# Four edits at once in a convolution and expert-lookup kernel: row halves in the first transform, a last quarter in two parts, fifteen score columns, and an index spread in two row tiles

## The chip, the cores and the metric

The kernel runs on one core of one Trainium2 chip. A core has a matrix engine (TensorE, PE in the profile, with its weight loads listed apart as PEld), a vector engine (VectorE, DVE), a scalar engine (ScalarE, ACT), a general engine (GpSimd, POOL), and a queue engine (SyncE, SP) that issues nearly all transfers of this kernel. The engines run their own instruction streams in order and wait for each other by semaphores. The metric is the device time of one execution in microseconds (us); lower is better.

## What is computed

The input is one sequence of 2048 positions with 512 channels. Two blocks follow each other, each on the normalised result of the one before, each added to its input:

```python
# block A: a state-space model as a long convolution
P = exp((A * dt)[:, :, None] * pos);  K = 2 * einsum("dn,dnl->dl", C, P).real
y = irfft(rfft(u, 2L) * rfft(K, 2L))[:L] + u * D_skip
# block B: 32 heads look up one of 256 experts for each position
q1, q2 = split(x @ w_q)                       # per head, 128 + 128
s1, s2 = q1 @ k1.T, q2 @ k2.T                 # 16 scores each
i1, i2 = argmax(s1), argmax(s2);  e = 16 * i1 + i2
out = sum over heads of gelu(x . u[e]) * v[e] # one candidate: the softmax is 1
```

## The kernel before

The program is a list of steps. Each step is added to a plan (`Plan.add`) with an engine, a cost, a function that issues its instructions, and the keys of data that it reads and writes. The order in which the steps are issued is the long tuple `ORDER`, written out by hand or by a search; the costs and lags in the plan do not act on the chip. Within an engine the steps run in the order of `ORDER`.

**Block A** handles the channels in four quarters, c = 0 to 3, and each quarter in four pieces kt.

- *Tables.* For each of 32 steps i, POOL makes phases (`phases`, L551) and magnitudes (`mags` L582, `tails` L588), with `steps`, `bases`, `powers` and `heads` once in four steps. ACT takes sines and cosines of the phases (L638 to L641), DVE multiplies (L645 to L658), and PE forms the convolution kernel from them (`kgen`, L684, tile `kps`). The tables have two buffers each, so `mags(i)` on POOL waits until `kgen(i-2)` has read its own.
- *Transforms.* `stage1` (L456 to L468) is the first factor of a Fourier transform, for the input (`u_s1`, tile `s1u`) and for the kernel (`k_s1`, tile `s1k`). For a piece it has two halves n. In each, for four g and two k, a matmul takes 128 rows of data (64 columns) as weights and moves `c1_s[:, k]`, 128 columns, of which only a block diagonal of four is not zero; k = 0 and 1 go to output partitions 0 to 63 and 64 to 127. ACT copies the bank out. `stage2` (L471 to L485, tiles `s2yu`, `s2yk`) is the second factor: eight steps k4 for a quarter, four matmuls of 128 x 128 weights and 128 columns each. `k_s2` multiplies the two spectra (DVE, L726 to L729; in the last quarter ACT, DVE and POOL share it, L733 and L737), and `k_ia` is the first inverse factor, eight steps n, 16 matmul records each (L758), copied to the tile `T` on ACT (in the last quarter ACT and DVE). In `k_s2` all eight steps wait for all four pieces of stage 1, and in `k_ia` all eight wait for all eight products.
- `yk` of one quarter takes the buffer that `yk` of the quarter before leaves after its `k_ia`.

**Between the blocks.** `w_piece(n)`, n = 0 to 31, multiplies the query weights with the keys `ka_s`, `kb_s` (load `wq`, L816; PE L822; turned by PE L830; ACT copies L826 and L834) and stores the product `w_d` in DRAM after every fourth piece (L837). It is read back as four tiles `w_q` and split into a high and a low part `w_hi`, `w_lo` (L914 to L918).

**Block B** goes through eight batches b of 256 positions: `inverse` (last inverse factor, L1029, then `h`), `center` and `variance`, `scores` for two halves of 128 positions, and `select`. In `scores`, four steps q of six matmuls give 1024 columns: 64 groups (32 heads, two keys) of 16 (L1143). DVE takes the maximum of each group (`top`, L1165), compares (`same`, L1169), multiplies the hits with powers of two (`weigh`, L1174); POOL adds the 16 up (`gather`, L1180); DVE reads the index from the exponent (`index`, L1187 to L1191). `select` turns the index of 32 heads (`ixt`, L1231), spreads it to 128 partitions by matmuls with the selector `sel` (`bc`, L1247: two matmuls of 32 rows for each of four banks), copies it out on ACT (L1251), compares it with the expert numbers on DVE (`oh`, L1269), counts (`cnt`, L1279) and multiplies with the values (`o`, L1316).

Of the kernel before, what the change touches and what calls it, by code (L numbers as in the profile page):

```python
# [9 lines left out]
F32 = mybir.dt.float32  # L10
# [9 lines left out]
P = 128  # L20
# [7 lines left out]
def view(t, off, dims):  # L28
# [135 lines left out]
def kernel(ctx, tc, xa, xb, xt, lar, aim, cre, cim, ldt, dsk, wq, ka, kb, ue, ve,  # L164
# [628 lines left out]
    def w_piece(n):  # L793
# [42 lines left out]
        def store():  # L836
            nc.sync.dma_start(w_d[:, :, 128 * hg:128 * hg + 128], W[hg])  # L837
# [598 lines left out]
```

## Time and profile before

| | |
|---|---|
| three runs | 508.86, 515.67 (median), 516.54 us |
| the profiled execution | 516.5 us, of which 514.7 us lie between the first and the last instruction (the span) |
| mean granted TensorE clock | 0.977 |
| busy, share of the span | PE 89%, DVE 80%, POOL 63%, ACT 58% |

A row of a group gives line, engine, operation, what is written and read, and the count; behind the bar stand the busy time of the group in us and the mean of one in ns, then the engine's idle time before them and what ended it. Matmuls overlap, so the mean of one is longer than the pace. Rows of the timeline and of the chain of waits give start, duration, and how many instructions they merge. A float32 matmul has two records on PE, each with a weight load on PEld. Rows of a table by stretch of time give, for each engine, busy time and number of instructions; then the granted clock, the share of the DMA engines and their rate.

### The profile page before, as it was taken

What the parts mean: (1) busy time and instruction counts of PE and PEld (TensorE: products, weight loads), DVE (VectorE), ACT (ScalarE), POOL (GpSimd) and SP (SyncE); (2) the same over time, 40 slices, a digit from 0 to 9 for tenths busy, and PEclk for the clock granted to TensorE, in tenths of its full rate; (3) what the DMA queues carried; (4) which work ended last, traced back from release to release, by engine and by line L of the source; (5) the groups of instructions that cost most, each with busy time, mean ns of one, the idle gap of its engine ahead of it and who ended that gap; (6) DMA issues with size and microseconds to landing.
All of it is one profiled execution on the core that took longest, in us unless ns stands there. A gap on an engine that the chain in (4) does not pass through costs nothing.

```text
span 514.7 us, 16728 instructions
## 1 busy us (share of the span) xinstructions
PE 459.3 (89%) x7206; PEld 392.3 (76%) x7206; DVE 411.3 (80%) x724; ACT 300.4 (58%) x596; POOL 321.7 (63%) x342
## 2 busy tenths in 40 slices
PE   0275889999999999999998949999999999999995
PEld 0143669888998999899997947877878888786784
DVE  5999898899959988999727573888969596979983
ACT  4867799967897598858964442334152341426240
POOL 4989979999999999996807011760351506263330
PEclk9998699999999999999999998999999999999998
DMA  7969474224043102611056984400162141010012
GB/s 255 385 206 383 127 276 146 65 84 175 3 177 96 40 3 82 202 50 44 1 208 183 292 266 155 144 1 1 54 186 91 30 137 42 1 43 0 2 42 85
DMA packets 27362, 61.32 MB, mean 119 GB/s; under 512 B 2932, under 2 KB 14456, under 8 KB 26136
## 3 DMA queue, kind: packets, MB, share of 16 engines
q1 hardware_dynamic: 27136, 60.11, 34.8%
q8 instruction: 57, 0.93, 0.8%
q10 hardware_dynamic: 152, 0.13, 0.1%
q14 instruction: 17, 0.14, 0.1%
HBM read 46.21 MB, written 14.02 MB: 117 GB/s over the span
## 4 chain that ended last, share of the span: by engine, by line
PE 62%; DVE 15%; ACT 11%; DMA 5%; issue 4%; POOL 2%; SPq 0%; DVEq 0%; ACTq 0%; POOLq 0%
PE sc L1143 18%; PE ia L758 8%; PE s2yk L482 4%; PE kps L684 4%; PE s1k L465 3%; PE xu L1150 3%; PE s2yu L482 3%; PE o L1316 3%; PE cnt L1279 3%; PE s1u L465 2%; PE ib L1029 2%; DMA wq<-wq 2%; ACT t L641 2%; PE bc L1247 1%; ACT t L639 1%
## 5 line engine op out<-in xcount | busy, mean ns | idle before, releaser
L551 POOL TENSOR_TENSOR pg<-PS 128x1024 int32<-128x1024 int32 x32 | 68.9, 2152 | 0.5
L582 POOL TENSOR_TENSOR mg<-TS 128x1024 f32<-128x1024 f32 x32 | 62.6, 1958 | 7.8 <-PE kps L684 4.1
L1180 POOL TENSOR_TENSOR ks<-kq 128x512 f32<-128x512 bf16 x16 | 18.9, 1182 | 56.6 <-DVE kq L1174 53.4
L1269 DVE TENSOR_SCALAR oh<-idxb,ec_s 128x2048 bf16<-128x2048 bf16 (+1 forms) x72 | 46.3, 708 | 8.9 <-ACT idxb L1251 7.0
L758 PE MATMUL ia<-ca_s,U 128*128 128x128 f32 x256 | 49.6, 276 | 0.0
L1053 POOL TENSOR_TENSOR vs<-hc 128x256 f32<-128x256 f32 x8 | 6.5, 815 | 62.5 <-ACT hc L1076 62.5
L1143 PE MATMUL sc<-w_hi,hhi 128*128 128x512 f32 x128 | 45.1, 434 | 0.0
L639 ACT ACTIVATE t<-t,halfpi 128x512 f32<-128x512 f32 x64 | 42.4, 662 | 2.1
L1143 PE MATMUL sc<-w_lo,hhi 128*128 128x512 f32 x128 | 40.8, 400 | 0.0
L638 ACT ACTIVATE t<-pg 128x512 f32<-128x512 int32 x64 | 38.9, 608 | 3.0 <-DVE gf L646 2.0
L1143 PE MATMUL sc<-w_hi,hlo 128*128 128x512 f32 x128 | 40.6, 399 | 0.0
L641 ACT ACTIVATE t<-pg 128x512 f32<-128x512 int32 x64 | 38.2, 608 | 3.2 <-POOL pg L551 2.1
L758 PEld LDWEIGHTS ia<-ca_s,U 128*128 128x128 f32 x256 | 38.9, 192 | 0.0
L758 PE MATMUL ia<-ca_s,yk 128*128 128x128 f32 x192 | 38.2, 281 | 0.4 <-DVE mg L658 0.4
L588 POOL TENSOR_TENSOR mg<-TS 128x512 f32<-128x512 f32 x32 | 37.4, 1171 | 0.4
L684 PE MATMUL kps<-mg 128*32 128x64 f32 x1024 | 34.0, 231 | 3.3 <-DVE mg L658 1.6
L465 PE MATMUL s1u<-c_s,xs 128*64 128x128 f32 x512 | 33.4, 277 | 2.5 <-DVE xs L502 1.6
L482 PE MATMUL s2yk<-yk,c_s 128*128 128x128 f32 x256 | 35.0, 283 | 0.5 <-DVE U L729 0.4
L684 PE MATMUL kps<-gf 128*32 128x64 f32 x1024 | 33.5, 228 | 0.9 <-issue 0.9
L482 PEld LDWEIGHTS s2yk<-yk,c_s 128*128 128x128 f32 x256 | 30.8, 192 | 3.7 <-issue 1.4
L465 PE MATMUL s1k<-c_s,k 128*64 128x128 f32 x512 | 32.8, 284 | 0.3 <-ACT yk L468 0.3
L482 PE MATMUL s2yu<-yu,c_s 128*128 128x128 f32 x256 | 32.6, 279 | 0.3
(197 smaller groups left out, 1380.9 us busy)
## 6 DMA issues: line engine op xcount, KB each, us to landing
wq<-wq SPq DMA_DIRECT2D x25, 512.0 KB, 4.1
t_d<-T SPq DMA_DIRECT2D x24, 256.0 KB, 4.2
Tb<-t_d SPq DMA_DIRECT2D x8, 768.0 KB, 6.0
x<-xa SPq DMA_DIRECT2D x8, 512.0 KB, 6.0
xs<-xb SPq DMA_DIRECT2D x16, 256.0 KB, 4.8
xt<-xt SPq DMA_DIRECT2D x8, 512.0 KB, 3.9
out<-ob SPq DMA_DIRECT2D x7, 512.0 KB, 3.0
c_s<-wq SPq DMA_DIRECT2D x4, 512.0 KB, 8.4
```

The lines of the kernel that those rows point to most:

```text
L465: T.matmul(ps[64 * k:64 * k + 64, g, :], lhs8(4 * n + g), c1_s[:, k], start=True, stop=True)
L482: T.matmul(ps[:, k, :], c2_s[:, kk, :], y[:, :, kk, :], start=True, stop=True)
L551: G.tensor_tensor(view(pg, 0, [[32, 2 * NC], [8, 4], [1, 8]]), view(t["PS"], 1024 + off, [[1, 2 * NC], [128, 4], [0, 8]]), view(t["PS"], 8 ...
L582: G.tensor_tensor(view(mg, 0, [[96, NC], [8, 8], [1, 8]]), view(ts, 512 + 8 * o, [[8, NC], [1, 8], [0, 8]]), view(ts, 8 * o, [[8, NC], [0, ...
L588: G.tensor_tensor(view(mg, 64, [[96, NC], [8, 4], [1, 8]]), view(ts, 1536 + o, [[1, NC], [64, 4], [0, 8]]), view(ts, 1024 + 8 * o, [[8, NC ...
L638: A.activation(p, pg[:, :, k], AF.Abs)
L639: A.activation(p, p, AF.Sin, scale=-SINSCALE, bias=halfpi)
L641: A.activation(p, pg[:, :, k], AF.Sin, scale=SINSCALE)
L684: T.matmul(kps[32 * q:32 * q + 32, 2 * g + h, :], m[:, d, 64:96], m[:, d, 0:64], start=(e == 0), stop=(e == 1))
L758: T.matmul(ps[:, g, :], t[:, 4 * n + g].rearrange("p a b -> p (a b)"), ca_s[:, s, :], start=(s == 0), stop=(s == 1))
L1143: T.matmul(ps[:, 512 * h:512 * h + 512], t[x_][:, q, ts], I[w_][:, q, 512 * h:512 * h + 512], start=(q == 0 and x_ == w_), stop=(q == 3 an ...
L1269: V.tensor_scalar(oh[:, :, 0:ln], t["idxb"][:, :, sl], S["ec"][:, 4 * e + j:4 * e + j + 1], None, op0=ALU.is_equal)
```

## The change

- **Stage 1 in row halves.** `c1_s` has 64 columns for each k in place of 128, a block diagonal of two. Each matmul of 128 rows becomes two of 64 rows (rows 0 to 63 and 64 to 127, h = 0 and 1), each moving 64 columns into its own bank. A piece takes both banks at once, and ACT copies each bank out after both halves of g.
- **The last quarter in two parts** (`SEGS = (1, 1, 1, 2)`). For c = 3, the steps k4 = 0 to 3 of `k_s2` handle the first two pieces kt and 4 to 7 the last two. A step has eight matmuls with 64 columns each in place of four with 128. `k_ia(3)` waits in its first four steps for the first four products alone.
- **Fifteen score columns.** POOL subtracts key 15 from the other fifteen (`differ`, two new operations that wait for the load of `ka_s`, `kb_s`), so the score of key 15 is zero and its column is dropped: 960 columns in place of 1024, matmuls of 480. DVE takes the larger of the maximum and zero (a new operation on 128 x 64), and the index formula is bounded from below so that no hit means 15. `gather` adds 0 to 7 and 7 to 14 with the weight of 7 halved.
- **Index spread in two row tiles.** `index` writes the index twice (64 columns), it is turned to 64 partitions, `sel` has two copies, and the eight matmuls of a batch come in two steps that alternate between rows 0 to 31 and 32 to 63, each with two banks.
- `ORDER` is new as a whole: 1712 steps in place of 1727. The keys of `params` were made stricter (`keyed`), which acts on the order alone. Some plan costs differ.

In the new `ORDER`, the weight pieces 26 to 31 stand ahead of `kgen(25)`; before, they stood among and behind the `s2yk` steps of the last quarter, ahead of `k_ia(3)`. In the last quarter the PE order is: stage 1 of kt 1, 0, 2; `kgen(30)`; `s2yk` 0 and 1; `kgen(31)`; `s2yk` 3; stage 1 of kt 3; `s2yk` 2, 4, 6, 5, 7; the eight `k_ia`. At the start, `aim` is loaded after the other five parameters (it was second), POOL begins with `differ`, `powers(0)`, `mags(1)`, and PE has weight pieces 0 to 10 ahead of `kgen(0)` (0 to 5, 7 and 9 before), 11 and 12 ahead of `kgen(1)`, up to 16 ahead of `kgen(2)` and up to 18 ahead of `kgen(3)`.

```diff
+        def differ():
+            for t, o in ((ka_s, 0), (kb_s, 16)):
+                G.tensor_tensor(t[:, o:o + 15], t[:, o:o + 15], t[:, o + 15:o + 16].to_broadcast([P, 15]), op=ALU.subtract)
+        plan.add("POOL", 0.6, differ, w=["ka"])
...
     def stage1(dst, lhs8, kt, nm, r, tiles, key):
...
-                ps = bank(job, f"{nm}_{n}")
-                for g in range(4):
+                if n == 0:
+                    for h in range(2):
+                        bank(job, f"{nm}_{h}", h)
+                for g in range(4 * n, 4 * n + 4):
                     for k in range(2):
-                        T.matmul(ps[64 * k:64 * k + 64, g, :], lhs8(4 * n + g), c1_s[:, k], start=True, stop=True)
+                        for h in range(2):
+                            hs = slice(64 * h, 64 * h + 64)
+                            T.matmul(flat(job[h], 64)[64 * k:64 * k + 64, g], lhs8(g)[hs], c1_s[hs, k], start=True, stop=True)
...
     def k_s2(c):
+        ns = SEGS[c]
         for k4 in range(8):
+            sg, nk = k4 * ns // 8, 4 * ns
+            g_, k_ = slice(32 * sg // ns, 32 * (sg + 1) // ns), slice(nk * (k4 % (8 // ns)), nk * (k4 % (8 // ns)) + nk)
+            kts = range(4 * sg // ns, 4 * (sg + 1) // ns)
...
+                for kk in range(k_.start, k_.stop):
+                    T.matmul(ps[:, kk - k_.start, :], c2_s[:, kk, :], spectrum(c, "yk")[:, g_, kk, :], start=True, stop=True)
...
-                    T.matmul(ps[:, 512 * h:512 * h + 512], t[x_][:, q, ts], I[w_][:, q, 512 * h:512 * h + 512],
+                    T.matmul(ps[:, 512 * h:512 * h + 480], t[x_][:, q, ts], I[w_][:, q, 480 * h:480 * h + 480],
...
+            V.tensor_scalar_max(d["mx"], d["mx"], 0.0)
+            V.tensor_tensor(eq, ps, d["mx"].rearrange("p (b g) -> p b g", b=2).unsqueeze(3).to_broadcast([P, 2, 32, 15]),
+                            op=ALU.is_equal)
...
+            a, b_ = (ef[:, :, j].unsqueeze(1).to_broadcast([P, 2, 32]) for j in range(2))
+            V.scalar_tensor_tensor(t[f"ix{k}"].rearrange("p (c h) -> p c h", c=2), a, 16.0, b_, op0=ALU.mult, op1=ALU.add)
...
+            for g in range(0, 8, 2 * hj):
...
                     for h in range(hj):
-                        T.matmul(bp[:, h], S["sel"][:, g + h, :], t["ixT"][:, sl], start=True, stop=True)
+                        for r in range(2):
+                            rs = slice(32 * r, 32 * r + 32)
+                            T.matmul(job[r][:, h], S["sel"][rs, g + hj * r + h, :], t["ixT"][rs, sl], start=True, stop=True)
```

More of the change, by code (lines that the diff above doesn't have):

```diff
@@ L180 @@
     e_d = dram.tile([P, 11, 256], F32, name="e_d")
-    w_d = dram.tile([P, 4, 1024], F32, name="w_d")
+    w_d = dram.tile([P, 4, 960], F32, name="w_d")
     I = {}
@@ L208 @@
     IA = (12, 12, 13, 13)
+    SEGS = (1, 1, 1, 2)
     US1 = ((0, 0, 0, 0), (0, 0, 1, 1), (9, 9, 10, 10), (17, 17, 18, 18))
@@ L370, in params, with keyed @@
         last = []
+        def keyed(ks, p):
+            return [(k, 0 if k in ("sg", "r64", "w0", "dt", "r") else p) for k in ks]
         def act(nm, p):
@@ L374, in act @@
             _, fn, r, w, tab = acts[p][nm]
-            n = plan.add("ACT", 0.5 if p else 0.15, fn, r=[(k, p) for k in r], w=[(k, p) for k in w], t=["pa", "pb"],
+            n = plan.add("ACT", 0.5 if p else 0.15, fn, r=keyed(r, p), w=keyed(w, p), t=["pa", "pb"],
                          tab=tab, after=last, take=("psA",) * 5 if (nm, p) == ("dt", 0) else ())
@@ L383, in dve @@
             cost, fn, r, w = dves[p][nm]
-            done[nm] = plan.add("DVE", cost, fn, r=[(k, p) for k in r], w=[(k, p) for k in w], t=["pa", "pb"], lag=0.1)
+            done[nm] = plan.add("DVE", cost, fn, r=keyed(r, p), w=keyed(w, p), t=["pa", "pb"], lag=0.1)
         def warm(fn, tab):
@@ L729, in prod, with part, rest @@
                     V.tensor_mul(uv[0:64], pv[64:128], uv[0:64])
-            def part(job=job, k4=k4):
-                job["ki"] = wk.tile([P, 128, 4], F32, tag="kt", name=f"ki{k4}", bufs=3)
-                A.copy(job["ki"][0:64], job["ps"].rearrange("p k m -> p m k")[64:128])
-            def rest(job=job, k4=k4):
-                uv = four(c, Q[c]["U"], k4).rearrange("p g d k -> p (g d) k")
+            def part(job=job, k4=k4, nk=nk):
+                job["ki"] = wk.tile([P, 512 // nk, nk], F32, tag="kt", name=f"ki{k4}", bufs=3)
+                A.copy(job["ki"][0:64], flat(job["ps"], 512 // nk).rearrange("p k m -> p m k")[64:128])
+            def rest(job=job, views=views):
+                pv, uv, kv = views()
                 G.tensor_tensor(uv[0:64], job["ki"][0:64], uv[0:64], op=ALU.mult)
+            k = plan.add("PE", 0.98 if ns == 1 else 1.15, mm, r=deps + u_k + ["c2"], t=tiles, take="psA", n_mm=8 * ns)
             if c < 3:
-                plan.add("DVE", 2.14, prod, r=[("U", c, k4)], w=[("P", c, k4)], t=tiles, give="psA", after=[k])
+                plan.add("DVE", 2.14, prod, r=u_k, w=[("P", c, k4)], t=tiles, give="psA", after=[k])
             else:
@@ L744, in k_s2 @@
                 a = plan.add("ACT", 0.52, part, w=[ki], t=[ki], after=[k])
-                v = plan.add("DVE", 1.43, prod, r=[("U", c, k4)], t=tiles, give="psA", after=[k, a])
+                v = plan.add("DVE", 1.43, prod, r=u_k, t=tiles, give="psA", after=[k, a])
                 plan.add("POOL", 1.5, rest, r=[ki], w=[("P", c, k4)], t=[ki, f"U{c}"], after=[v])
@@ L749, in k_ia @@
         plan.group = f"ia{c}"
-        deps = [("P", c, k4) for k4 in range(8)]
         for n in range(8):
-            job = {}
+            job, sg = {}, n * SEGS[c] // 8
+            deps = [("P", c, k4) for k4 in range(8 * sg // SEGS[c], 8 * (sg + 1) // SEGS[c])]
             def mm(n=n, job=job):
@@ L776, in k_ia @@
             else:
-                a = plan.add("ACT", 0.70, lambda turn=turn: turn(A.copy, 0), w=[("T", c, n, 0)], t=[f"T{c}"], after=[k])
-                plan.add("DVE", 0.70, lambda turn=turn: turn(V.tensor_copy, 1), w=[("T", c, n, 1)], t=[f"T{c}"], give="psA",
+                a = plan.add("ACT", 0.75, lambda turn=turn: turn(A.copy, 0), w=[("T", c, n, 0)], t=[f"T{c}"], after=[k])
+                plan.add("DVE", 0.75, lambda turn=turn: turn(V.tensor_copy, 1), w=[("T", c, n, 1)], t=[f"T{c}"], give="psA",
                          after=[k, a])
@@ L1155, in scores @@
         for q in range(4):
-            last = plan.add("PE", 1.48, lambda q=q: mm(q), t=tiles, after=[] if last is None else [last],
+            last = plan.add("PE", 1.40, lambda q=q: mm(q), t=tiles, after=[] if last is None else [last],
                             r=[(x, k) for x in tiles] + [("w_hi", q), ("w_lo", q)], take="psC" if q == 0 else None, n_mm=6)
@@ L1195, in gelu @@
             A.activation(act[:, k], jx["ps"], AF.Gelu_apprx_tanh, scale=t["rstd"][:, k:k + 1])
-        a = plan.add("DVE", 1.15, top, w=[m], t=[m], after=[last])
-        plan.add("DVE", 1.15, same, r=[m], w=[e], t=[m, e], give="psC", after=[a])
-        plan.add("DVE", 0.62, weigh, r=[e, "cst"], w=[kq_], t=[e, kq_], lock=True)
+        a = plan.add("DVE", 1.08, top, w=[m], t=[m], after=[last])
+        plan.add("DVE", 1.17, same, r=[m], w=[e], t=[m, e], give="psC", after=[a])
+        plan.add("DVE", 0.58, weigh, r=[e, "cst"], w=[kq_], t=[e, kq_], lock=True)
         plan.add("POOL", 2.8, gather, r=[kq_], w=[s_], t=[kq_, s_])
@@ L1299, in select @@
             if ln == 256:
-                plan.add("ACT", 0.52, high, r=[("wt", p)], w=[("whi", p)], t=[kA, kH])
+                plan.add("ACT", 0.64, high, r=[("wt", p)], w=[("whi", p)], t=[kA, kH])
                 plan.add("DVE", 0.62, low, r=[("wt", p), ("whi", p)], w=[("wlo", p)], t=[kA, kH, kL], lock=True)
@@ L1376, in _constants @@
     e = np.arange(16)
-    keys = np.tile(np.concatenate([2.0 ** (15 - e)] * 2)[None], (128, 1))
+    key = 2.0 ** (15 - e[:15])
+    key[7] /= 2
+    keys = np.tile(np.concatenate([key] * 2)[None], (128, 1))
     ecode = 136.0 - (32 * np.arange(8)[None, :] + (np.arange(128) % 32)[:, None])
```

114 lines of the change are left out of this document (61 added, 53 removed), and 161 rows, old and new, of the table ORDER.

## Prediction

> **What bounds the kernel now.** I read the table by stretches of time first, then the chain of waits, then single groups and timeline rows for prices.
>
> ```profile
> span 514.7 us, 16728 instructions
> ...
> 80.00:215.00 135.00, 132.22 (x2588) 122.16 (x2587) 117.81 (x194) 112.81 (x215) 131.62 (x121) 1.00 0.28 94
> 215.00:256.00 41.00, 40.64 (x643) 37.99 (x632) 36.36 (x60) 31.82 (x60) 35.10 (x31) 1.00 0.17 53
> 256.00:280.00 24.00, 22.25 (x426) 19.40 (x424) 13.74 (x22) 13.91 (x31) 9.64 (x8) 1.00 0.58 190
> 280.00:299.00 19.00, 15.63 (x171) 15.19 (x174) 9.67 (x23) 10.29 (x23) 0.49 (x1) 1.00 0.84 264
> ...
> 310.00:505.00 195.00, 192.51 (x2251) 153.98 (x2250) 155.82 (x235) 69.55 (x116) 76.40 (x106) 0.99 0.20 64
> ```
>
> Columns: length; busy us of PE, PEld, DVE, ACT, POOL; clock; DMA share; GB/s. From 80 to 215 PE (132.2 of 135) and POOL (131.6) are both full: making PE faster alone gains nothing there. From 215 to 256 PE is full and POOL loses 5.9; from 256 POOL has done its tables. From 310 on PE is busy 192.5 of 195, DVE 155.8: block B belongs to PE.
>
> ```profile
> 254.72 1.17 POOL L588 TENSOR_TENSOR mg<-TS 128x512 f32<-128x512 f32 x1
> ...
> 258.50 0.69 DVE L658 TENSOR_TENSOR mg<-mg,t 128x512 f32<-128x512 f32 x1 [0.63 <-ACT t L639]
> ...
> POOL mg L582 <- PE kps L684: 4.1, 2, 2.8
> ...
> 262.22 3.67 PE s1k L465 x64
> ...
> 265.92 0.59 ACT yk L468
> ...
> 272.16 0.57 PE wps L822 x16
> 272.74 0.26 PE wpt L830
> ...
> 274.63 4.00 DMA wq<-wq
> ...
> 281.02 3.44 DMA w_d<-wh
> ...
> 285.34 7.31 DMA w_q<-w_d
> ...
> 298.62 1.43 PE ib L1029 x85
> ...
> 304.77 4.99 issue
> ...
> 310.19 2.01 PE sc L1143 x4
> ```
>
> POOL's last table piece ends at 255.9, DVE's last product on it at 259.2. From there 39 us pass until block B's first matmuls (`ib`, 298.6): stage 1, then `s2yk` mixed with late weight pieces, one of which waits for its load (274.6), then their store and the reading back as `w_q` (281 to 292.7), and the copies of `T`. Another 11.6 us, 5 of them a stand of PE without a shown cause, lie before the first score (310.2). The profiled execution took 516.5 us, 1.8 beyond its span and 0.8 above the median 515.67; the sum goes against it and 0.8 comes off at the end.
>
> **Stage 1 in row halves.**
>
> ```profile
> L465 PE MATMUL s1u<-c_s,xs 128*64 128x128 f32 x512 | 33.4, 277 | 2.5 <-DVE xs L502 1.6 <-ACT yu L468 0.9
> ...
> 257.55 3.64 PE s1k L465 x64
> ...
> 256.52 1.03 PE kps L684 x64
> ...
> 487.93 0.52 PEld L1117 LDWEIGHTS var<-ones_d,vs 128*128 128x128 f32 x4 [0.21 <-issue]
> ...
> L1117 PEld LDWEIGHTS var<-ones_d,vs x32: 186/192/193, 315.8 to 488.3; 128*128 128x128 f32 x32
> ```
>
> Two pieces of `s1k` take 3.64, so a piece (32 records of 128 columns, 64 wide) takes 1.82, 57 ns a record. The new piece has 64 records of 64 columns in four tiles of the array, two by rows and two by columns. The nearest row is `kps`: 64 records, 64 columns, four column tiles, 1.03, each with its own weight load. No row has two row tiles at work, so the bounds are wide: 1.03 if row tiles overlap as column tiles do, 3.65 (64 x 57) if nothing overlaps. The `var` row gives the pace of weight loads where the matmul is one column: its four loads, each 0.19 long, fill 0.52, a pitch of (0.52 - 0.19)/3 = 0.11 for 128 columns, so 0.055 for 64. Should two row halves of one column strip load in turn, a group of four would take 0.11 and a piece 1.75: no gain. I take 1.05, because `kps` has the same number of records and loads. The saving is 0.77 a piece, on 32 pieces 25 us of PE.
>
> The Trainium skill, page "TensorE: Matmul & The Clock Gate", section "LDWEIGHTS (loading the stationary operand)", speaks against this edit: a load takes columns / 1.2 ns whatever the rows, so halving rows saves nothing on a load and there are twice as many; `var` agrees with its pace (107 by the page as an estimate). Its other rule, "TensorEngine Tiling (Array Packing)", section "Key Properties", lets different tiles load and multiply in parallel; by the first alone, loads in turn, a piece would take 64 x 53 ns = 3.4 us, and the sum about 536 (by the second rule 489); `kps` contradicts that for column tiles, and for row tiles no row here shows it.
>
> A piece now takes two banks at once and its copies wait for all its matmuls, half a piece (0.5) more of delay, which I count only where a piece is on the path, at the end; the ACT copies (0.59) keep their 512 elements, and ACT has 22 of 135 us free.
>
> By `ORDER` some 22 of the pieces (twelve `s1u`, ten `s1k`) lie between 80 and 256, so PE gets 17 us back there. It uses 5 for weight pieces 26 to 31 (0.57 + 0.26 each), which move ahead of `kgen(25)`, and 3 for stage 1 of the last quarter. PE falls to about 94% and POOL becomes the bound. Hence of 17 us only POOL's waits come back: 4.1 for `kps`, and of the remaining idle (1.8 in the second stretch, 3.4 in the first) I count 2.3.
>
> **POOL's new work and the start.**
>
> ```profile
> L574 POOL TENSOR_TENSOR TS<-Mg,E 128x64 f32<-128x64 f32 x8 | 2.6, 327 | 0.0
> ...
> 1.19 5.05 DMA pa<-aim
> ...
> 30.00:40.00 10.00, 6.68 (x124) 4.17 (x116) 9.69 (x19) 7.63 (x18) 9.92 (x9) 1.00 0.51 152
> ...
> 34.80 0.66 PE L822 MATMUL wps<-wq,ka_s 128*32 128x128 f32 x8
> ...
> 44.78 6.62 DMA wq<-wq
> ...
> 55.60 1.86 PE kps L684 x64
> ```
>
> `differ` is two small operations, 2 x 0.33 = 0.7 at the head of POOL's queue, where it waits for the keys; behind it stand `powers(0)` and everything of the tables. `aim`, on the chain before, lands later, but POOL now does `powers` and `mags(1)` first, which don't need it; I cost the start at nothing, with ends of -2 and +8 (the rival below). Tables end at 255.9 - 6.4 + 0.7 = 250.2.
>
> **The last quarter in two parts, and the weight pieces gone from behind it.**
>
> ```profile
> 170.66 0.89 PE s2yk L482 x8
> ...
> 246.16 5.55 PE ia L758 x48
> ...
> 268.36 0.69 DVE L726 TENSOR_TENSOR yu<-s2yk,U 128x512 f32<-128x512 f32 x1 [5.28 <-ACT ki L733]
> ...
> 279.18 0.68 DVE L727 TENSOR_TENSOR U<-s2yk,U 64x512 f32<-64x512 f32 x1
> ...
> 279.23 1.26 POOL L737 TENSOR_TENSOR U<-ki,U 64x512 f32<-64x512 f32 x1 [0.18 <-DVE yu L726]
> ```
>
> An `s2yk` step is 8 records in 0.89. Split, it has 16 records with full 128-column loads and 64 columns to move: 0.89 if the columns set it, 16 x 0.11 = 1.75 if the loads do. I take 1.75, as `var` shows loads that cannot go faster. The eight products took 268.4 to 279.9, 1.44 each; an `ia` step 1.85. Forward from 250.2: DVE's last product 3.3 later, 253.5; `kgen(31)` 254.5; `s2yk` 3 to 256.3; stage 1 of kt 3 to 257.3 and its copies to 258.5; five `s2yk` steps to 267.2 (DVE's eight products alone would reach 265.0); last product and POOL's share 269.9, beside which the first four `ia` run from 267.2 to 274.6; the other four to 282.0; copies to 283. `T` stood ready at 298.6, so this gives -15.6. The reading back of `w_q` needs only the tables' end now, and its 12 us fit ahead of 283. If the load bound is wrong, five steps get 4.3 shorter.
>
> Of the stand at 304.8 I count 3 of 5 as gone: it fell in a stretch of heavy transfers that now start earlier. The ends are 0 and 5.
>
> **Fifteen columns and the index spread, in block B.**
>
> ```profile
> 356.07 1.40 PE sc L1143 x6
> ...
> 352.14 0.97 PE bc L1247 x8
> ...
> L1169 DVE TENSOR_TENSOR eq<-sc,mx 128x1024 bf16<-128x1024 f32 x16 | 19.5, 1221 | 0.3
> ...
> L1174 DVE TENSOR_TENSOR kq<-eq,key_s 128x1024 bf16<-128x1024 bf16 x16 | 11.2, 704 | 0.2
> ...
> L1187 DVE TENSOR_SCALAR ei<-ks 128x64 int32<-128x64 int32 x16 | 3.9, 246 | 3.2 <-POOL ks L1182 3.2
> ```
>
> A score step of six matmuls takes 1.40; a sixteenth less is 0.0875, on 64 steps 5.6. The spread takes 0.97 a batch; paired by row tiles 0.49, on 8 batches 3.9, or nothing if they don't pair. On DVE the comparison loses 0.076 (1.22/16), the maximum as much, and the new maximum with zero costs up to 0.25 by the `ei` row, in the path that frees the score banks: +0.1 x 16 = 1.5 if PE waits for it. `kq` keeps 0.70 or, if rows of 30 lose its fast rate, goes to about 1.2, 8 us more on DVE, which has 39 us of slack in this stretch. Longer `index` writes lie in that slack. Together -8 (ends -9.5 and -2).
>
> Sum: -15.6 - 3 - 8 = -26.6; 516.5 - 26.6 = 489.9, less 0.8 gives **489**.
>
> **The rivals.**
> *Early weight pieces hold the tables back.* PE now has pieces up to 18 ahead of `kgen(3)`, which ran at 55.6. Pieces pass through two buffers; piece 9 ran at 34.8, and four pairs at 6.6 (the `wq` row) behind 9 and 10, say from 38, put `kgen(3)` at 64.5. POOL's table buffers then shift the whole table phase by about 6, as POOL has no slack to make it up: 495 (489 to 501). For it: POOL is full. Against: the transfer engines were busy only 0.51 from 30 to 40, so loads can come earlier.
> *Row halves load in turn.* Stage 1 stays at 1.75, PE stays full to 256 with 5 us of weight pieces added, so the tables end no earlier: 489 + 6 (the tables' end) + 5 (weight pieces on a full PE) + 2 (0.7 for each of three pieces near the end) = 502 (497 to 509). For it: the 0.11 pitch of `var`. Against: `kps`.
> *Slower: row and column tiles serialise.* At 57 ns a record a piece costs 3.65, 1.83 more; on the 26 pieces after 80, where PE is full, that is 48. My sum without stage 1's gain (6) plus 48 is 543. It is slower than before from 2.6 us a piece ((26.6 - 6)/26 above 1.82). Against: pairs and fours of column tiles already overlap in `s1k` and `kps`.
>
> **How the numbers follow.** The likeliest case has 56 in 100, its own range 480 to 498 (`s2yk` at 0.89, the stand kept or gone, block B's ends). Early pieces 18, loads in turn 16, serialised tiles 7, and 3 for less than 480. The range 478 to 506 leaves out the serialised case, the top of the third and a little below. About 2% (10.3 us, 505.4 and 526) is what a measurement here tells from no change; faster holds the first, nearly all of the second and half of the third case: 0.83, within 0.10, slower 0.07.
>
> **What would show it.** Right: `s1k` and `s1u` 64 records in about 1.05; last `tails` near 250; `s2yk` of the last quarter 16 records in 1.75; the first `ib` near 283 and the first score near 291; six score matmuls in 1.31, the spread in 0.5. Wrong: stage 1 at 1.75 or more, `kgen(3)` past 60 with POOL waiting for `kps` early, or PE idle in block B behind the score banks.

## The result and the profile after

The changed kernel took 519.46 us (median of 20 runs, 515.73 to 521.9) against 514.64 of the kernel before (20 runs, 508.86 to 517.75): a ratio of 1.0114, interval 1.0084 to 1.0144. It is 1.1% slower; 489 was forecast. The profiled execution took 515.9 us, of which 514.1 are its span, at the lower end of its runs; before it was 516.5 and 514.7, in the upper part of its runs, so the two profiles side by side do not show the 1.1%. Ratios compare executions of the faster state of the chip alone, and the profiled executions of two trials below, e6 and e13, are of the slower one, 6 us above their medians, so that places and waits read from these two carry that much more doubt.

The table by stretches, columns as before (length; busy us of PE, PEld, DVE, ACT, POOL; clock; DMA share; GB/s), of the changed kernel:

```profile
span 514.1 us, 18917 instructions
...
80.00:215.00 135.00, 120.03 (x2924) 108.94 (x2918) 114.11 (x188) 108.60 (x209) 125.21 (x117) 0.97 0.34 109
215.00:256.00 41.00, 35.67 (x930) 32.23 (x923) 32.97 (x52) 30.24 (x58) 33.62 (x31) 1.00 0.16 60
...
313.00:508.00 195.00, 184.47 (x2270) 153.29 (x2270) 166.61 (x253) 75.13 (x121) 79.06 (x109) 1.00 0.20 69
```

PE, full before from 80 to 215 (132.2 of 135), stands 15 us there now, and POOL, nearly as full (131.6), does only 125.2 us of work. The tables come later although PE has less to do. Single rows, from the timeline, the chain of waits, the list of waits, the instruction queue and the groups:

```profile
268.65 1.17 POOL L602 TENSOR_TENSOR mg<-TS 128x512 f32<-128x512 f32 x1
...
280.07 1.02 PEld L477 LDWEIGHTS s1k<-c_s,k 64*64 64x64 f32 x64
280.07 1.16 PE L477 MATMUL s1k<-c_s,k 64*64 64x64 f32 x64
...
278.14 2.00 PE L739 MATMUL s2yk<-yk,c_s 128*128 128x64 f32 x16
...
304.58 0.31 PE L1057 MATMUL ib<-cb,Tb 128*32 128x64 f32 x6
...
306.39 0.24 PE L1057 MATMUL ib<-cb,T 128*32 128x64 f32 x1 [0.58 <-DVE T L798]
...
382.83 0.54 PE bc L1285 x8
...
388.77 1.30 PE sc L1171 x6
...
POOL mg L596 <- PE kps L698: 18.7, 11, 5.1
...
q8 instruction: 65, 1.06, 0.9%
```

Stage 1 does what was hoped: 64 records in 1.16 (before 1.82 for 32). The last table piece ends at 269.8 (before 255.9); POOL's wait for `kps` ahead of `mg` is 18.7 in all from 20 to 285 (before 4.1). From the last table piece to the first score, at 312.8, pass 43.0 us (forecast 41.4, before 54.2). The row of `ib` at 298.6 that the forecast took for the first matmuls of block B is not the first in the timeline before: six of them stand at 294.81, and the others wait for copies of `T` until 298.62.

```profile
294.81 0.31 PE L1029 MATMUL ib<-cb,Tb 128*32 128x64 f32 x6
...
298.62 0.24 PE L1029 MATMUL ib<-cb,T 128*32 128x64 f32 x1 [1.59 <-DVE T L771]
```

The row like that one stands at 306.39 now: 36.6 us behind the tables (forecast 32.8, before 42.7), and 6.4 ahead of the first score (forecast 8.6, before 11.5). Block B, from the first score to the last instruction, takes 197.9 (before 201.2, forecast 193.2). The score step has 1.30, the spread 0.54.

So the miss on the profiled execution, 515.9 against 489.9, lies in two places: 19.6 us at the tables' end, 4.7 in block B, and some 2 between them. The experiments take these two apart.

### The profile page after: what moved, and what is told of

Read it like the earlier page. It is cut to its first block, busy times and chain, and to the rows that moved or that the text cites. A ratio compares the mean times of both kernels' runs of the same rounds, so it can differ in the third digit from the quotient of the medians.

```text
span 514.1 us, 18917 instructions
## 1 busy us (share of the span) xinstructions
PE 439.5 (85%) x8294; PEld 378.6 (74%) x8294; DVE 425.6 (83%) x740; ACT 306.4 (60%) x600; POOL 322.4 (63%) x344
## 5 line engine op out<-in xcount | busy, mean ns | idle before, releaser
L596 POOL TENSOR_TENSOR mg<-TS 128x1024 f32<-128x1024 f32 x32 | 62.5, 1953 | 18.9 <-PE kps L698 18.7
L1308 DVE TENSOR_SCALAR oh<-idxb,ec_s 128x2048 bf16<-128x2048 bf16 (+1 forms) x72 | 48.2, 725 | 5.9 <-ACT idxb L1291 5.9
L1171 PE MATMUL sc<-w_hi,hhi 128*128 128x480 f32 x128 | 43.0, 417 | 0.2 <-DVE eq L1203 0.2
L739 PE MATMUL s2yk<-yk,c_s 128*128 128x128 f32 (+1 forms) x320 | 41.3, 280 | 2.2 <-DVE U L755 1.6
L739 PEld LDWEIGHTS s2yk<-yk,c_s 128*128 128x128 f32 x320 | 37.6, 192 | 4.1 <-PE s1u L477 1.8
L1171 PE MATMUL sc<-w_hi,hlo 128*128 128x480 f32 x128 | 38.4, 381 | 0.0
L1171 PE MATMUL sc<-w_lo,hhi 128*128 128x480 f32 x128 | 38.4, 381 | 0.0
L785 PEld LDWEIGHTS ia<-ca_s,yk 128*128 128x128 f32 x192 | 29.1, 191 | 4.6 <-DVE U L755 1.8
L667 DVE TENSOR_TENSOR mg<-mg,t 128x512 f32<-128x512 f32 x32 | 21.8, 683 | 11.9 <-ACT t L653 11.8
L496 PEld LDWEIGHTS s2yu<-yu,c_s 128*128 128x128 f32 x256 | 29.9, 192 | 2.3 <-ACT wh L861 1.2
```

The costliest lines, as they stand in the source:

```text
L496: T.matmul(ps[:, k, :], c2_s[:, kk, :], y[:, :, kk, :], start=True, stop=True)
L596: G.tensor_tensor(view(mg, 0, [[96, NC], [8, 8], [1, 8]]), view(ts, 512 + 8 * o, [[8, NC], [1, 8], [0, 8]]), view(ts, 8 * o, [[8, NC], [0, ...
L739: T.matmul(ps[:, kk - k_.start, :], c2_s[:, kk, :], spectrum(c, "yk")[:, g_, kk, :], start=True, stop=True)
L785: T.matmul(ps[:, g, :], t[:, 4 * n + g].rearrange("p a b -> p (a b)"), ca_s[:, s, :], start=(s == 0), stop=(s == 1))
L1171: T.matmul(ps[:, 512 * h:512 * h + 480], t[x_][:, q, ts], I[w_][:, q, 480 * h:480 * h + 480], start=(q == 0 and x_ == w_), stop=(q == 3 an ...
L1308: V.tensor_scalar(oh[:, :, 0:ln], t["idxb"][:, :, sl], S["ec"][:, 4 * e + j:4 * e + j + 1], None, op0=ALU.is_equal)
```

## The experiments

A kernel "in the old order" issues the steps in the list of the kernel before; a step whose data or bank is not there yet moves back until it is. Ratios are to the kernel before, run on the same chip. "Tables" is the end of the last table piece on POOL in the profiled execution, "block B" the time from the first score to the last instruction there. "The last instruction" is the last that keeps an engine busy.

| | median us | ratio (interval) | tables | block B |
|---|---|---|---|---|
| before | 514.64 | 1 | 255.9 | 201.2 |
| changed | 519.46 | 1.0114 (1.0084 to 1.0144) | 269.8 | 197.9 |
| e1 all edits, old order | 538.9 | 1.0457 (1.0419 to 1.0496) | 284.1 | 193.7 |
| e2 changed, old start | 523.27 | 1.0119 (1.0058 to 1.018) | 272.6 | 197.6 |
| e3 before, new start | 521.98 | 1.0136 (1.0059 to 1.0212) | 265.2 | 198.2 |
| e4 row halves, old order | 545.9 | 1.0603 (1.0581 to 1.0625) | 285.9 | 199.5 |
| e5 the same, halves adjacent | 538.25 | 1.0408 (1.0348 to 1.0468) | 272.2 | 201.6 |
| e6 all edits, halves adjacent | 537.43 | 1.0271 (1.0207 to 1.0335) | 273.7 | 193.5 |
| e7 old order, new last quarter | 544.04 | 1.0526 (1.0472 to 1.058) | 299.5 | 192.5 |
| e8 changed, old weight places | 545.57 | 1.0545 (1.0477 to 1.0613) | 299.1 | 199.4 |
| e9 two banks, old matmuls | 527.1 | 1.0291 (1.0214 to 1.0368) | 265.8 | 200.5 |
| e10 changed without row halves | 529.69 | 1.0351 (1.0271 to 1.0432) | 281.1 | 197.9 |
| e11 fifteen and spread, old order | 505.0 | 0.9837 (0.9746 to 0.9929) | 255.0 | 192.3 |
| e12 changed, old block B | 514.18 | 1.0038 (0.9992 to 1.0084) | 271.4 | 193.3 |
| e13 twice the records, old banks | 524.01 | 1.0217 (1.0133 to 1.0302) | 265.6 | 201.6 |
| e14 changed without the split | 534.07 | 1.0438 (1.0357 to 1.0519) | 271.8 | 199.9 |
| e15 fifteen columns, old order | 509.85 | 0.9902 (0.9847 to 0.9956) | 255.5 | 195.4 |
| e16 spread, old order | 513.28 | 0.9986 (0.9936 to 1.0036) | 255.7 | 198.8 |
| e17 as e11, five rounds | 504.68 | 0.9837 (0.9763 to 0.9911) | 254.7 | 193.9 |
| e18 e11 with the split | 530.52 | 1.036 (1.0297 to 1.0424) | 255.1 | 195.9 |

### First theory: the new order holds the tables back

**e1, all edits in the old order.** Only the list differs from the changed kernel:

```diff
-ORDER = (new list)
+ORDER = (list of the kernel before, steps matched by name)
```

> All edits of the change (row halves, halved last quarter, fifteen columns, two copies of the indices), but issued in the order of the kernel before: only the written-out order differs from the changed kernel. Theory 1, the new order (five weight pieces more ahead of the third table, eight more ahead of the tenth) starves POOL and costs the table phase 14 us: POOL's last table piece ends at 251 to 258 (before 255.9, changed 269.8), kgen(3) runs near 55, time 495 to 508. Rival A, the edits themselves slow PE's stream (1,024 stage-1 records issued instead of 512, two banks held by each piece): the last table piece ends at 264 or later under this order too and the time is 515 or more. Theory 3 on block B (DVE's new maximum and slower small operations eat what PE saves): block B, from the first score to the last instruction, lasts 197 to 199 as in the changed kernel, not 193.

Tables at 284.1, 538.9 us: the theory's numbers fall in the table phase, and the rival's stand, though with two flaws of the trial. Under the change's stricter keys the old list delays two parameter steps, so `kgen(0)` runs at 40.0 and not 36.9; and in the old list other work stands between the two halves of a piece. Block B came out at 193.7: not the 197 to 199 of theory 3, but the forecast's 193.2 nearly.

**e2, the old start in the changed kernel.**

```diff
-ORDER = (new list)
+ORDER = (old list up to kgen(8), then what is left of the new list)
```

> The changed kernel, but all that the kernel before issues up to kgen(8) is issued first and in that order; the rest follows in the new order. Theory 1: kgen(2) and kgen(3) run at 50 and 55 as before, kgen(8) near 92 (before 92.3, changed 102.5), and of the 14 us by which the tables ended late 8 to 10 go; time 505 to 511. If the later weight pieces and stage-1 pieces alone hold POOL back, kgen(8) is early but the last table piece still ends at 266 or later and the time stays at 515 or above. Rival A: kgen(8) is late by itself, 98 or more.

`kgen(8)` ran at 97.6 (changed 102.5), and yet the tables ended at 272.6. Five us gained at the start (with the flaw of e1) did not reach the end, which is the second expectation's case: POOL waited 22.0 us for `kps`.

**e3, the new start in the kernel before.**

```diff
-ORDER = (old list)
+ORDER = (new list up to kgen(8), then what is left of the old list)
```

> The kernel before, but all that the changed kernel issues up to kgen(8) is issued first and in that order. Theory 1: kgen(3) runs at 64 or later, the last table piece ends 7 to 14 us later than before (263 to 270) and the time is 520 to 530. Rival A: the order alone costs nothing, kgen(8) near 92 and the time within 3 us of the kernel before.

As the theory had it: `kgen(3)` at 64.2, tables at 265.2, 9.3 later than before. The new start costs that much where the rest is as before; 6.5 us of it reach the time.

**e4, row halves alone in the old order.**

```diff
 SEGS = (1, 1, 1, 1), sixteen columns, one copy of the index, old list
+stage1 as in the change
```

> Row halves of stage 1 alone, in the order of the kernel before. Theory 1: a piece takes 1.0 to 1.1 us against 1.82, POOL gets its waits on kps back, the last table piece ends at 250 to 256 and the time is 508 to 515. Rival A (issue of twice the records, two banks held from the first half on): the tables end at 260 or later, time over 520.

545.9 us: 30 slower than before. Waits of e4 from 80 to 285 (what waits, for what: us in total, times, longest):

```profile
ACT yu L490 <- PE s1u L485: 19.7, 11, 3.5
DVE mg L675 <- ACT t L661: 13.5, 11, 2.2
POOL mg L604 <- PE kps L706: 12.9, 9, 4.7
```

ACT is to empty both banks behind the second half, that half stands behind other work of PE, and ACT works in order: the sines for the next tables (`t`) wait, then DVE, then POOL. That is the flaw of e1 seen at work, and a hint: the latency of a piece matters here, not its PE time.

**e5 to e7.** e5 mends both flaws (the halves of a piece adjacent, the parameter steps with the old keys):

```diff
 order: ... s1mm0, [other work], s1mm1 ...
+order: ... s1mm0, s1mm1, [other work] ...
```

> Row halves of stage 1 alone in the order of the kernel before, as in the first trial of them, but the two halves of a piece issued one behind the other, so that no other work of PE stands between them while both banks are held and ACT waits (there ACT waited 25 us for stage 1), and with the parameter stage in exactly the old order (kgen(0) at 36.9 again, not 40). If the split pieces were what cost 30 us: the last table piece ends at 250 to 258 and the time is 508 to 515. Rival (two banks a piece and twice the records cost PE by themselves): the tables still end at 264 or later, 520 or more.

The start was the old one (`kgen(0)` at 36.5), and still the tables ended at 272.2: the rival's case. Row halves cost 16 us in the order that served the kernel before.

e6 is all edits in that order, e7 the same with the last eight weight pieces earlier and the new last quarter:

```diff
 e7: old list up to kgen(28)
+    w24..w31 behind kgen(20)..kgen(27); new list up to sc0_1q0; old list in block B
```

> All edits of the change in the order of the kernel before, halves of a piece issued one behind the other. If the edits are sound and only an order that was laid out for them loses the gain: tables end at 250 to 258, block B lasts 193 to 195 as in the first trial of this (193.7), time 500 to 508, below the kernel before. If the edits themselves cost the table phase: tables end at 264 or later and the time is over 515.

> All edits; the order of the kernel before up to kgen(28) with the last eight weight pieces spread behind kgen(20) to kgen(27), then the new order for the last quarter up to the first score steps, then the old order in block B. If the start and the middle of the new order lose what stage 1 gives, and its block B loses 4 us, this is the fastest: tables end 252 to 258, from there 43 us to the first score as in the changed kernel, block B 193 to 195, time 492 to 500. If row halves keep POOL waiting in any order: tables end 264 or later and 510 or more.

Both went the rival's way in the table phase (273.7 and 299.5). In e7 the moved pieces made it worse: from 180 to 285 PE waited 5.1 us at one stroke for DVE's `gf` and 4.4 for ACT's copy of a weight piece. In both, block B stayed short, at 193.5 and 192.5.

**e8, the weight pieces alone put back.**

```diff
-new list: w14..w23 ahead of kgen(2) to kgen(10)
+each of them behind the step that it follows in the old list
```

> The changed kernel, but weight pieces 14 to 23 go to the places among the other work that they have in the kernel before (five of them ahead of kgen(3) and five ahead of kgen(10) go behind). Theory 1, pieces of weight work ahead of the tables hold POOL back: kgen(3) at 58 to 60 (changed 64.1), kgen(10) at 112 to 118 (changed 124.0), last table piece 260 to 265 (changed 269.8), time 507 to 512. Rival (PE waits on ACT, DVE and its instructions in the middle wherever the pieces stand): kgen(10) gains less than 3 us, the last table piece ends at 267 or later, time 515 or more.

The first theory does not come out here. `kgen(3)` gained 2.7 (61.4), `kgen(10)` lost 2.8 (126.8), and the tables ended at 299.1. The trial is no clean test of it, for at their new places PE waited 14.4 us from 20 to 285 for the loads of weight pieces; a list that moves the loads along was not tried.

### What row halves cost

Row halves bring three things: less PE time, two banks held to the end of a piece, and twice the records. e9 takes the second without the others, though with the halves of a piece moved together as in e5; e13 takes the third alone. Both have 1.8 us of PE for a piece.

**e9.**

```diff
     def stage1(...):
+        both banks taken ahead of n = 0
         for n in range(2): the 16 matmuls of 128 rows, as before, into bank n
-        each bank emptied behind its half
+        both banks emptied behind n = 1
+order: the halves of a piece adjacent, as in e5
```

> The kernel before with its own stage-1 matmuls (128 rows, 1.82 us a piece), but a piece takes both its banks before its first half and ACT empties both only behind its second half, as row halves need it; order as in the trial of row halves with adjacent halves. Theory 4, holding two banks of seven until the end of the piece (not the matmuls) starves PE, ACT and DVE: PE stands idle 20 us or more between 80 and 285 (before 5), the last table piece ends at 268 or later and the time is 530 or more. Rival B (twice as many PE instructions run dry, or the pairs themselves): PE idle under 10 us, tables end at 256 to 262, time 515 to 522.

Tables at 265.8, 9.9 later, though PE did its old work: between the two expectations for the place, and PE's idle time too (12.3 of 205 by the stretches below; 5.1 before). What the adjacent halves cost by themselves was not tried, so the 9.9 is for the two together.

**e10, the changed kernel with the old stage 1**, each half emptied at once:

```diff
-stage1 in row halves
+stage1 as before, in the new list; each eviction directly behind its half
```

> The changed kernel in its own order, but stage 1 as before: 128 rows, 1.82 us a piece, one bank per half, each half emptied as soon as it stands. PE gets 20 us more work in stage 1. If row halves gain anything in the order laid out for them, this is slower: tables end at 275 or later, 520 or more. If their bank hold and their bursts of instructions cost as much as they save (theory 4 or rival B), it is the same or faster: tables end at 262 to 270, 508 to 516, and PE's waits without a cause in the profile fall from 8.6 us between 80 and 285 to about 2.

529.7 us: in the list that was laid out for them, row halves gain 10 to 12 us (by the medians and by the ratios), the tables 11.3. And the waits that the profile gives no cause for are gone. PE's waits from 80 to 285 in the changed kernel, where they stand:

```profile
PE kps L698 <- issue: 4.6, 5, 1.8
PE s1k L477 <- DVE k L710: 3.0, 3, 1.9
PE s1u L477 <- issue: 2.6, 3, 0.9
PE s2yk L739 <- DVE U L755: 1.6, 2, 1.0
PE ia L785 <- DVE U L755: 1.6, 1, 1.6
PE s1k L477 <- issue: 1.3, 1, 1.3
```

"issue" is a wait for nothing that the profile shows: 8.5 us here, 0.9 before, none in e10.

**e13, twice the records and nothing else**: each stage-1 matmul cut into two column tiles.

```diff
-    T.matmul(ps[64 * k:64 * k + 64, g, :], lhs8(4 * n + g), c1_s[:, k], ...)
+    for j in range(2):
+        m = 64 * k + 32 * j
+        T.matmul(ps[m:m + 32, g, :], lhs8(4 * n + g)[:, 32 * j:32 * j + 32], c1_s[:, k], ...)
```

> The kernel before, but each stage-1 matmul cut into two of 32 columns of the stationary operand (1,024 records of 128x32 instead of 512 of 128x64, 128 columns moved in each), one bank per half and the old order: twice the instructions without the second bank and without shorter pieces. Theory 5a, the count of PE instructions outruns their supply by itself: PE's waits without a cause rise from 1 to 5 us or more between 80 and 285, the last table piece ends at 262 or later, 521 or more. Theory 5b, only bursts as short as row halves (64 records in 1.05 us ahead of and behind other short work) do that: a piece still takes 1.75 to 1.9, waits stay under 2, tables end at 255 to 259, 514 to 519.

524.0 us, 8.5 more than before in the medians, and tables at 265.6, 9.7 later, with one bank per half and the old order. PE's waits from 80 to 285 in e13, and its instruction queue:

```profile
PE kps L701 <- issue: 4.3, 3, 2.6
PE s1u L481 <- issue: 2.8, 2, 2.6
PE s1k L481 <- issue: 1.7, 1, 1.7
...
q8 instruction: 65, 1.06, 0.8%
```

8.8 us of waits without a cause, with no row tiles in it: they go with the count of records and not with the row tiles. The other traces agree. From 80 to 285 these waits are 0 to 1.2 us in the nine traces with 512 matmuls in stage 1 (the expectation calls them records; each has two). In the eleven with 1,024 they are 4.6 to 8.8 in eight (e5: 7.1) and 0 to 2.7 in three. The queue that carries instructions moved 65 packets of 16 KB here and in the changed kernel, 57 before. In the two traces PE stands sixteen times between 80 and 285 for 0.66 us or more inside stage 1, inside a `kgen` or between the two. Three of these end late after a DVE or ACT operation; the other thirteen ended 1.2 to 1.6 us after such a packet had ended. That PE waits there for its own instructions is read from this, and nothing else was tried. The Trainium skill, "Runtime: NRT & Kernel Launch", section "Instruction fetch mechanics", says that an engine's instructions come in blocks of 16 KiB, 256 instructions, and that crossing a block is mostly hidden. The kernel before agrees (0.9 us). With 1,024 matmuls in stage 1 the crossing is not hidden, if the reading above is right.

The second bank has a page too: "TensorEngine Tiling (Array Packing)" of the Trainium skill, section "Gotcha 1: PSUM Pressure", says that row tiles write to different banks and press on them. In this kernel the tables end 9.9 us later in e9, where both banks are held.

The stretch from 80 to 285 in the kernel before, in e5, in e9, in e13 and in e10, in that order:

```profile
80.00:285.00 205.00, 199.91 (x3681) 184.36 (x3677) 168.76 (x275) 159.85 (x309) 176.85 (x159) 1.00 0.30 99
```

```profile
80.00:285.00 205.00, 175.96 (x4368) 162.28 (x4372) 157.88 (x257) 153.69 (x286) 166.28 (x151) 0.94 0.24 82
```

```profile
80.00:285.00 205.00, 192.70 (x3585) 178.05 (x3585) 163.16 (x265) 156.02 (x296) 170.57 (x155) 0.99 0.27 88
```

```profile
80.00:285.00 205.00, 192.88 (x4455) 179.29 (x4447) 163.06 (x266) 156.65 (x298) 171.96 (x155) 0.98 0.27 90
```

```profile
80.00:285.00 205.00, 189.54 (x3504) 172.24 (x3504) 162.59 (x267) 156.61 (x301) 173.18 (x155) 1.00 0.26 87
```

Before, PE stands 5 us in these 205; with row halves 29, with the banks or the records alone 12 each. The granted clock is lower too, 0.94 in e5, and this is a cost of its own. Two rows of e5, and one stretch with its clock:

```profile
221.18 0.46 PE L703 MATMUL kps<-gf 128*32 128x64 f32 x8
...
227.89 0.28 PE L703 MATMUL kps<-gf 128*32 128x64 f32 x8
```

```profile
220.80:227.60 6.80, 6.18 (x204) 5.65 (x196) 5.63 (x10) 5.45 (x10) 6.64 (x8) 0.50 0.15 45
```

Between 80 and the tables' end e5 has four such stretches at 0.50, 20 us together, in which PE was busy for 18.4. As the rows took nearly twice as long in them, an estimate from these numbers is that they cost PE some 9 us. The kernel before has no such stretch there, e9 one of 3.4 us and e13 two; what brings them was not tried.

In the old order the bank with the adjacent halves costs 9.9 at the tables' end and the records 9.7 there (8.5 in the time, by the medians); with both and the shorter pieces it is 16.3 (e5). So the 21 us less PE work of these pieces (32 at 1.82 against 32 at 1.16) would be worth 2 to 3 there if the two costs add and nothing else differs; the stretches at 0.50 say that something else does.

### The last quarter

**e14, the changed kernel without the split.**

```diff
-    SEGS = (1, 1, 1, 2)
+    SEGS = (1, 1, 1, 1)
```

> The changed kernel without the split of the last quarter: its stage-2 steps have 8 records of 128 columns again and wait for all four of its pieces, its inverse steps for all eight products; order otherwise the new one. If the split gave the 11 us from the last table piece to the first score, that stretch lasts 50 us or more again instead of 43 and the time is 523 or more. If the weight pieces moved ahead of it gave them: 42 to 46 us, and the time within 3 us of the changed kernel, 517 to 522.

From the last table piece to the first score 56.1 us instead of 43.0, and 534.1: the split gives 13 in the new list, which was laid out for it.

**e18, the split in e11**, with weight pieces 26 to 31 at their old places:

```diff
 stage1 as before, SEGS = (1, 1, 1, 2)
+old list up to kgen(30), new list up to sc0_1q0 with w26..w31 where the old list has them, old list after
```

> The same, with the last quarter split and issued from kgen(30) to the first score steps in the new order, but with weight pieces 26 to 31 among its steps at the places they have in the kernel before; stage 1 as before. If the split by itself gives the gain: from the last table piece to the first score 43 to 47 us instead of 52, 496 to 501. If it needs PE free of the weight pieces: 52 or more, 504 or more.

76 us from the last table piece to the first score: on the side of the second expectation, but far beyond its 52. Waits of e18 from 255 to 345:

```profile
PE mean L1119 <- DVE h L1069: 21.1, 1, 21.1
...
DVE w_lo L951 <- ACT w_hi L950: 12.7, 2, 12.3
...
ACT w_hi L950 <- DMA w_q<-w_d: 10.7, 1, 10.7
```

DVE's queue has all four steps of splitting `w_q` ahead of the first `h` in the new list (three of them before); with the weight pieces late, they wait for the reading back, and block B's first step waits behind them. In this list the split needs the early weight pieces.

### Block B

**e11, e15, e16: the two edits of block B in the old order**, together and alone (e17 is e11 again in five rounds).

```diff
 stage1 and SEGS as before, old list
+e15: fifteen columns;  e16: index spread in two row tiles;  e11, e17: both
```

> Fifteen columns and the spread in two row tiles alone, in the order of the kernel before; stage 1 and the last quarter as before. The table phase should stand as before (last table piece 255 to 257, the first score at 310 to 312) and block B should last 193 to 195 (before 201.2, changed 197.9): 507 to 510. If the new maximum and the writes of twice the index cost DVE's path what PE saves: block B 198 or more, 513 or more.

> Fifteen columns alone in the order of the kernel before. By the sum of the prediction they give 5.6 us in the score steps less up to 1.5 for the new maximum: block B 196 to 198 (before 201.2), time 509 to 512. If DVE's new maximum costs more than that: block B 199 or more, 513 or more.

> The spread in two row tiles alone in the order of the kernel before. By the sum of the prediction it gives 3.9 us: block B 197 to 198, time 510 to 512. If the writes of twice the index on DVE and the pairs of banks cost what the paired matmuls save: block B 200 or more, 513 or more.

> The kernel of the eleventh trial once more (fifteen columns and the spread alone, order of the kernel before), in five rounds: 503 to 508, a ratio of 0.978 to 0.988 with an interval of half the width.

Block B 192.3 with both (193.9 in e17), 195.4 with fifteen columns, 198.8 with the spread: 8.9 (7.3), 5.8 and 2.4 us less than in the one trace before. Six traces with the old block B in the old list (before, e3, e4, e5, e9, e13) lie between 198.2 and 201.6, so the 2.4 is within what traces differ by. Together the edits give 504.7 us, a ratio of 0.9837 (0.9763 to 0.9911): this version beats both kernels, and by a little more than was expected (507 to 510). Fifteen columns alone took the time that was expected. The spread came out between its two expectations, and by itself it is not told from no change in the time.

**e12, the changed kernel with the old list in block B.**

```diff
-new list
+new list up to sc0_1q0, old list after
```

> The changed kernel up to the first score step of block B, from there the order of the kernel before. If the new order of block B gives back what fifteen columns and the spread save: block B lasts 193 to 195 instead of 197.9 and the time falls by 3 to 5 us. If DVE's operations set it in any order: 197 or more and the time of the changed kernel within 2 us.

193.3 instead of 197.9, and 514.2: 4 to 5 us less than the changed kernel (by the ratios and by the medians) for the same edits. Over all traces with both edits, block B takes 192.3 to 195.9 with the old list there (seven) and 197.6 to 199.9 with the new one (five). The small operations of the index in the changed kernel, and in e12 (the tile's view: shortest, median and longest in ns, and who waited for it):

```profile
L1223 DVE TENSOR_SCALAR ef<-ei x16: 194/725/1019, 330.2 to 496.7; 128x64 f32<-128x64 int32 x16
L1226 DVE SCALAR_TENSOR_TENSOR ix<-ef x16: 225/796/812, 330.4 to 496.9; 128x64 bf16<-128x64 f32 x16
...
  PE ixt L1266: 4.6, 7
```

```profile
L1236 DVE TENSOR_SCALAR ef<-ei x16: 195/196/1018, 335.9 to 494.2; 128x64 f32<-128x64 int32 x16
L1239 DVE SCALAR_TENSOR_TENSOR ix<-ef x16: 224/226/957, 336.6 to 494.4; 128x64 bf16<-128x64 f32 x16
...
  PE ixt L1279: 0.6, 1
```

In both traces every `ef` and `ix` that had no POOL operation beside it took 195 and 225; beside one most took 600 to 1,020 and 800. In the new list 11 of 16 `ef` lie beside POOL, in the old one 8, and PE waits 4.6 us for `ix` in place of 0.6. That the list moves these operations beside POOL and that block B is 4.6 longer go together here; that the one makes the other was not tried apart.

## Why the prediction was wrong

- **Stage 1 at 1.05 us a piece** was right: 64 loads in 1.02, the matmuls in 1.16 with their modelled end, and the tiles overlap as those of `kps` do.
- **Tables' end at 250.2 (255.9 - 6.4 + 0.7)** is the step that failed; it was 269.8. The step kept the tables' old place under a new list, and took the time freed on PE as time given back to POOL ("Hence of 17 us only POOL's waits come back: 4.1 for `kps`"). POOL's wait for `kps` did not go but rose to 18.7. With row halves alone in the old order the tables end 16.3 later and not 6.4 earlier (e5). The prediction counted the second bank only as half a piece of delay at the end, where e9 has 9.9 with the adjacent halves, and the second set of records at nothing, where e13 has 9.7.
- **"I cost the start at nothing, with ends of -2 and +8"**: the new start cost 9.3 where it was tried alone (e3), above the upper end, and `kgen(0)` ran at 41.8 and not 36.9. Yet the old start, put back into the changed kernel, gave nothing (272.6, e2).
- How these costs share the 13.9 us in the changed kernel itself stays open. Taken row halves first, they cost 16.3 in the old order (e5) and the rest gives 2.4 back; taken the other way, the new list with the old stage 1 ends its tables 25 us later than before (e10), and row halves then gain 11.3, more than the forecast's 6.4. That list was laid out for the short pieces, so its 25 is no fair price of the order. An order searched with these prices was not tried.
- **The rival of early weight pieces** had its sign right and `kgen(3)` at 64.1 (forecast 64.5). Putting ten pieces back took 2.7 of the 8.6 us away there, but made the kernel 4% slower than the changed one (e8), so its reason is not shown.
- **Row halves that load in turn** and **tiles that serialise** did not occur: beside the 1.16 at the full clock, a piece that took 1.83, from 84.6 us, ran mostly where the clock was 0.50. The serialised tiles were the only case that the prediction had for a slower kernel.
- **The last quarter** was right in its sum: 43.0 from the tables' end to the first score, where 41.4 was forecast (before 54.2). Its two terms missed in opposite ways: `T` was ready 36.6 behind the tables (32.8 forecast), and the way from there to the score was shorter than forecast (6.4 against 8.6). The split step has 16 records in 1.86 of loads (1.75 forecast). Its gain depends on the split (13 us, e14) and on the early weight pieces (e18).
- **Block B at -8** was right for the edits, -8.9 in the old order (e11; -7.3 in e17), with 5.8 for the columns (5.6 less up to 1.5 forecast) and 2.4 for the spread (3.9). The new maximum took 0.31 us in the mean in the changed kernel and 0.25 in e11, where the bound was 0.25. What failed is that the sum kept the old order's waits: the new list gave back 4.6 (e12).

## What to carry to other kernels

Here two engines were both full and waited for each other in turn, and less work on one was worth little in the old order; ask first which latency the other waits for, and price an edit by the banks that it holds and the instructions that it adds as well as by its time on the engine. A written-out order belongs to the durations that it was laid out for: try edits first in the old order, one by one, and keep those that gain there (here two of four, 1.6%). An edit that loses in the old order and gains in the new is not judged by either alone.

## What the runs showed of the hardware

- Twice as many matmuls in stage 1, each half as wide, for the same products cost 2.2% (1.3 to 3.0, e13): PE's waits without a cause from 80 to 285 went from 0.9 to 8.8 us.
- Row tiles of 64x64 with four in the array ran 64 records of 64 columns in 1.16 us, near the 1.03 of four column tiles of 128x32 (`kps`).
- The DVE operations `ef` and `ix` on 128x64, 0.2 us alone, took 0.6 to 1.0 beside a POOL operation in most cases, so their place in the order is worth more than their size.
- The granted clock was 0.94 over the 205 us of e5 in which PE stood for 29, and 1.00 before, where it stood for 5. In stretches at 0.50, 8 records of `kps` took 0.46 us, beside them 0.28.
